# Cluster-masked attention with a SiLU feed-forward layer on one core: eight small DMAs issued from ScalarE's queue in place of SyncE's

## The chip, the cores and the metric

The kernel runs on one core of one Trainium2 chip. The metric is device time in microseconds (us) of a whole execution, given as the median of several runs. Beside the timed runs there is one profiled execution; its times are counted from its first instruction.

Names of engines: PE is TensorE's matmul side and PEld its weight loads, ACT is ScalarE, DVE is VectorE, POOL is GpSimd, SP is SyncE. An engine's name with a q behind it (SPq, ACTq) is its instruction queue, from which it also issues DMAs.

## The reference

Four batches, eight heads, 768 positions, 64 dims per head. Every query and key gets the cluster (of 16) whose normalised centroid it agrees with most, and a query attends only to the keys of its own cluster. The attention output goes through a feed-forward layer with SiLU.

```python
q_assign = np.argmax(np.einsum('bhsd,hcd->bhsc', q_n, c_n), axis=-1)
k_assign = np.argmax(np.einsum('bhsd,hcd->bhsc', k_n, c_n), axis=-1)
mask = q_assign[:, :, :, None] == k_assign[:, :, None, :]
scores = np.where(mask, scale * np.matmul(q, k.transpose(0, 1, 3, 2)), -1000000000.0)
attn = softmax(scores);  x = attn @ v          # x: 3072 x 512
h = x @ w_in;  out = (h / (1 + exp(-h))) @ w_out
```

## The kernel before

**How the mask is made.** A head of a batch is a job; jobs 8 to 15 are the eight heads of batch 1 (names h8 to h15). A job's queries and keys are loaded (`raw`), split into a high and a low half (`hl`: `hi` on ACT, DVE or POOL, `lo` on DVE), and turned over by a DMA transpose (`xpose`, step `ht`) into the tile `ab`, whose 128 rows are the 64 rows of the high half and 64 of the low half. From `ab` PE makes the logits against the centroids (`l` or `L`), DVE takes their maximum (`mx`) and compares (`ge`), which gives a one-hot code for each position. PE turns the codes over (`cd_mm`, step `cm`), and `cd_ev` (step `ce`) takes them out of PSUM into a small tile `cd` of 96 partitions, scaled, with a constant added on the keys' side. From there a DMA of 48 KB moves them into rows 64 to 79 of `ab`. That DMA is the move that the change is about. A single matmul of `ab` by `ab` (`qk_mm`) then gives the score and the mask's penalty at once.

**What waits for a move.** `qk` of a head is the first that reads the moved rows. PE makes the scores of half a head's queries against a third of its keys per step (`qk0` to `qk191`) into `pS`, of which there are two. ACT takes the exponential of each (`ex0` to `ex191`), into `P`. So `qk` of n+2 waits until `ex` of n has read its scores. ACT also does the `tanh` of the feed-forward units (step `t`), some of the evictions, and some `hi`. The feed-forward units (`e`: PE into `ph`, then `t` on ACT, `g` on DVE) and `qk` are interleaved on PE. A `ph` bank comes free when `g` has read it.

**What sets the order.** The order on every engine is that of a list of words, `plan`, written out by hand. Every word is a step, with the engine's letter behind a dot (A ACT, D DVE, P POOL) and a PSUM bank. The list is walked once; each step appends its instructions to its engine's queue, and each queue runs in order. So an instruction that waits holds everything behind it on its engine.

**DMA semaphores.** Each DMA from SP or ACT counts on one of eight semaphores (DMAHW0 to DMAHW7 in the listings), given out in turn over both queues. Before a DMA is issued, its queue waits until the DMA that had the same semaphore before has landed. Here I call such a semaphore a lane.

**The eight moves.** In batch 1 the evictions of jobs 8, 10, 9, 14 and 15 run on ACT and those of 11, 12 and 13 on DVE; all eight moves are issued by SP, among the loads (`raw`, `vn`), the transposes and the stores of results. (Batch 0's moves, which come earlier, are issued by SP as well; batches 2 and 3 make their codes in another way, with moves issued by POOL on line 212.)

Of the kernel before, what the change touches and what calls it, by code (L numbers as in the profile page):

```python
# [29 lines left out]
def kernel(  # L30
# [10 lines left out]
    nc = tc.nc  # L41
    B, H, S, D = q.shape
    HC = centroids.shape[1]
# [39 lines left out]
    raws, hls, abs_ = {}, {}, {}  # L83
# [141 lines left out]
    def cd_ev(job, eng):  # L225
        m = (job.n + 1) // 2
        cd = mp.tile([6 * HC, 256], f16, name="cd", bufs=4)
        psN = psNs.pop(job.name)
        o, i = cd[0 : m * HC], psN[0 : m * HC, 256:512]
        add = 0.0 if job.name[0] == "x" else kadd[0 : m * HC, m - 5 : m - 4]  # L230
        if eng == "A":
            nc.scalar.activation(out=o, in_=i, func=AF.Identity, bias=add, scale=OHV)
        else:
            nc.vector.tensor_scalar(out=o, in0=i, scalar1=OHV, scalar2=add, op0=ALU.mult, op1=ALU.add)  # L234
        nc.sync.dma_start(abs_[job.name][64 : 64 + HC, 0 : 2 * m, :].rearrange("p n c -> p (n c)"), o)

    def ct_mm(job, banks):
        for part, lo_, n, bk in (("q", 6, 3, banks[0]), ("k", 0, 6, banks[1])):
# [365 lines left out]
    def step(op, n, eng, banks):  # L604
# [38 lines left out]
        elif op in ("cm", "xc"):  # L643
            cd_mm(job if op == "cm" else xj, bk)
        elif op in ("ce", "xe"):
            cd_ev(job if op == "ce" else xj, eng)
        elif op == "ct":
            ct_mm(job, banks)
# [86 lines left out]
        ex33 t14 g14 qk34 t8 ex34 qk35 e11.2 e13.3 ht10 g8 wc4 wc5 t11 g11 r12 ex35 t13 g13 qk36 ex36 e10.1 e15.0 qk37  # L735
        pt4.2 qk38 e2.3 t10 ex37 ex38 lo11 pe4.D ht9 r14 pv5.2 g10 t15 nm5 qk39 qk40 t2 ex39 ex40 e7.1 e12.2 t12 ht11
        g15 qk41 ex41 t7 g2 r15 wc6 e9.0 qk42 t9 b0.3 qk43 g7 b1 ex42 wc0 qk44 g12 g9 hi13.D L8.1 ex43 b2 qk45 lo13
        mx8 L10.2 ge8 cm8 mx10 ex44 b3 ex45 ce8.A wc1 ge10 bo0 pv6.1 nm6 qk46 l9.0 ht13 cm10 vl15 ls9 mx9 wc2 ge9 qk47
        hi12.A lo12 vl13 ht12 wc12 b4.3 ce10.A ex46 pt6.2 b5 cm9.0 ex47 hi14.A ce9.A pe6.A lo14 r16 pv7.1 nm7 b6 ht14
        pt5.0 pe5.D qk48 hi15.D lo15 ht15 v10.D pt7.1 pe7.A r17 ex48 b7 bo1 e24.0 e18.1 t24 g24 t18 L11.2 wc8 mx11 g18  # L740
        ge11 e22.3 t22 hi16.P e21.0 t21 g22 v11.D v8.D g21 qk49 qk50 cm11 ce11.D ex49 ex50 l12.3 vl9 ls12 e29.1 r18
        t29 g29 e20.0 t20 g20 e27.2 v13.A mx12 t27 g27 e23.3 ge12 qk51 t23 ex51 l13.1 ls13 qk52 ex52 g23 mx13 e19.0
        t19 e25.2 g19 t25 cm12.1 qk53 ex53 e26.3 g25 v15.D qk54 t26 ex54 ce12.D vl16.P g26 e16.0 t16 e30.2 qk55 ge13
        g16 vl17.P l15.3 ls15 t30 ex55 lo16 r20 qk56 e28.0 t28 ex56 vl14 g30 e17.3 g28 L14.1 qk57 qk58 t17 g17 ex57
        cm13.2 mx14 e31.0 ce13.D ex58 qk59 t31 v9.D mx15 S3 m1.3 ge14 od2 hi17.A ex59 g31 ge15 wc13 pv8.2 cm14 lo17
        r19 ce14.A ht17 qk60 nm8 ex60 S1 qk61 ex61 m7 qk62 ex62 cm15.0 ce15.A wc7 S13 pv9.1 z0 qk63 ex63 S2 nm9 wc14
        v16.D wc9 wc15 wc10 qk64 m11.2 ex64 qk65 m2.0 qk66 ex65 m17 ex66 hi18.P qk67 qk68 lo18 z10 ex67 ht16 vl21.P
        wc11 wc3 S11 v17 S4 m6 pv10.1 ex68 z1 hi20.D qk69 ex69 qk70 ex70 m5 o0 qk71 ex71 l17.0 S12 m16 z2 nm10 z11
        ls17 qk72 vl19.P ht18 vl18.P hi19.A xd8 qk73 l16.0 od1 o3 ex72 r22 r21 ex73 m4 mx17 m15 z12 ls16 mx16 lo19
# [46 lines left out]
    for word in plan:  # L796
        name, *rest = word.split(".")
        eng = rest[0] if rest and rest[0].isalpha() else None
# [31 lines left out]
```

## Time and profile before

| | |
|---|---|
| time, median of 3 runs | 299.18 us (299.0 to 299.66) |
| span of the profiled execution, first to last instruction | 297.9 us |
| what lies around the span (median less span; the profiled execution's own time is not listed beside its span) | 1.3 us |
| PE busy | 288.7 us, 97% |
| PE weight loads busy | 212.6 us, 71% |
| ACT busy | 233.2 us, 78% |
| DVE busy | 223.8 us, 75% |
| POOL busy | 68.7 us, 23% |
| granted TensorE clock | 1.000 |
| moves `ab<-cd` on SP | 16 in the kernel, 8 of them in batch 1 |

How to read it: the share of busy time is an average over the whole kernel. Batch 1's codes are made and moved between 62 and 99 us, so what the change does is read from that stretch. SP does nothing but wait and issue DMAs; its rows show how long its queue was held by each DMA's issue, and a DMA lands some time after.

### The profile page before, as it was taken

To read this page: it belongs to the slowest core of one execution; us is meant where nothing else is said; L and a number is where in the kernel's file an instruction comes from. 1 tells how busy PE (TensorE), PEld (TensorE's weight loads), DVE (VectorE), ACT (ScalarE), POOL (GpSimd) and SP (SyncE) were. 2 spreads that over 40 slices of the span, in tenths; PEclk is the share of its full clock that TensorE was granted. 3 is DMA by queue.
4 is the path that set the end of the run, shared out by engine and by line. 5 is a ranking of instruction groups with operands and counts; after the bars stand their busy time and mean duration, and the time that the engine had idled before them with its cause. 6 is when DMAs were issued, how large, how long until landed. Compare 5 with 4: busy or idle time off the path is not lost.

```text
span 297.9 us, 8577 instructions
## 1 busy us (share of the span) xinstructions
PE 288.7 (97%) x3433; PEld 212.6 (71%) x3433; DVE 223.8 (75%) x489; ACT 233.2 (78%) x406; POOL 68.7 (23%) x124
## 2 busy tenths in 40 slices
PE   7899999999979999999999999999999999999995
PEld 3767766666658887777866887767867886777684
DVE  5898849689979986989467897788656733666663
ACT  5998999965979878999789876898669768964731
POOL 2655804000227001334444024220420000000000
PEclk9999999999999999999999999999999999999999
DMA  6999999999997899795399535867221102211103
GB/s 214 286 256 247 179 201 176 193 247 216 171 300 178 171 176 257 176 151 131 102 202 213 164 66 114 256 165 113 51 89 35 26 2 74 82 29 35 39 19 125
DMA packets 75208, 44.13 MB, mean 148 GB/s; under 512 B 54288, under 2 KB 70960, under 8 KB 75168
## 3 DMA queue, kind: packets, MB, share of 16 engines
q1 hardware_dynamic: 70272, 35.75, 50.3%
q0 software_dynamic: 4608, 7.54, 13.5%
q8 instruction: 27, 0.44, 0.6%
q10 hardware_dynamic: 288, 0.30, 0.3%
q14 instruction: 13, 0.11, 0.1%
HBM read 27.30 MB, written 6.29 MB: 113 GB/s over the span
## 4 chain that ended last, share of the span: by engine, by line
PE 87%; DMA 5%; ACT 3%; DVE 3%; issue 1%; SPq 0%; ACTq 0%
PE ph L390 25%; PE pS L325 20%; PE xb L477 18%; PE pO L342 12%; PE psN L159 4%; PE yb L477 3%; PE po L417 2%; DMA ab<-cd 2%; DMA ab<-hl 1%; DMA raw<-in_q_dram 1%; DVE hl L112 1%; PE wb L477 1%; ACT P L330 1%; ACT hl L103 1%; PE pTq L135 1%
## 5 line engine op out<-in xcount | busy, mean ns | idle before, releaser
L330 ACT ACTIVATE P<-pS 128x768 f16<-128x768 f32 x192 | 151.0, 815 | 18.8 <-PE pS L325 17.4
L390 PE MATMUL ph<-xt,win_s 128*128 128x384 f16 x512 | 96.1, 326 | 0.0
L405 DVE SCALAR_TENSOR_TENSOR gt<-tn,ph 128x384 f16<-128x384 f32 x128 | 68.2, 549 | 31.9 <-ACT tn L402 31.0
L325 PE MATMUL pS<-ab 128*128 128x384 f16 x384 | 86.7, 326 | 2.2 <-DMA ab<-cd 1.6
L402 ACT ACTIVATE tn<-ph 128x384 f32<-128x384 f32 x128 | 61.6, 499 | 13.9 <-PE ph L390 10.5
L390 PEld LDWEIGHTS <-win_s 128*128 128x128 f16 x512 | 49.4, 98 | 31.0 <-issue 0.3
L325 PEld LDWEIGHTS <-ab 128*128 128x128 f16 x384 | 34.2, 98 | 18.3 <-DMA ab<-cd 2.2
L342 PEld LDWEIGHTS <-P 128*128 128x128 f16 x1152 | 39.8, 97 | 3.8 <-DVE cd L234 0.4
L342 PE MATMUL pO<-vt,P 128*128 128x65 f16 x1152 | 41.2, 193 | 0.0
L477 PEld LDWEIGHTS <-gt 128*128 128x128 f16 x352 | 34.1, 98 | 6.5
L112 DVE SCALAR_TENSOR_TENSOR hl<-raw,hl 128x768 f16<-128x768 f32 (+3 forms) x35 | 32.0, 916 | 0.8 <-ACT hl L103 0.5
L105 POOL TENSOR_SCALAR hl<-raw 128x768 f16<-128x768 f32 (+1 forms) x9 | 19.5, 2167 | 47.2 <-DVE gt L405 30.7
L477 PEld LDWEIGHTS <-s 128*128 128x128 f16 x264 | 25.5, 98 | 4.7
L199 POOL TENSOR_SCALAR od<-od 128x96 f16<-128x96 f16 x16 | 8.4, 526 | 63.3 <-DVE od L192 63.2
L499 ACT ACTIVATE ot<-xb 128x256 f32<-128x256 f32 x33 | 12.7, 385 | 12.9 <-PE xb L477 12.6
L477 PE MATMUL xb<-wout_s,gt 128*128 128x256 f16 x176 | 22.6, 273 | 0.0
L159 PEld LDWEIGHTS <-ab 128*128 128x128 f16 x544 | 18.9, 97 | 4.1 <-DMA ab<-hl 0.5
L477 PE MATMUL xb<-wc,s 128*128 128x256 f16 x160 | 20.7, 272 | 0.0
L159 PE MATMUL psN<-stk,ab 128*128 128x16 f16 (+1 forms) x544 | 20.1, 184 | 0.1
L354 DVE TENSOR_TENSOR xn<-pO,zr 128x384 f16<-128x384 f32 x32 | 17.8, 557 | 1.1
L490 DVE TENSOR_TENSOR s<-gt 128x1024 f16<-128x1024 f16 x22 | 15.5, 712 | 1.3 <-PE xb L477 1.0
L212 POOL DMA_DIRECT2D ab<-cdt x16 | 9.0, 564 | 19.8 <-PE pS L325 5.2
(93 smaller groups left out, 258.2 us busy)
## 6 DMA issues: line engine op xcount, KB each, us to landing
raw<-in_k_dram SPq DMA_DIRECT2D x31, 192.0 KB, 3.9
raw<-in_q_dram SPq DMA_DIRECT2D x24, 192.0 KB, 3.5
out_dram<-ot SPq DMA_DIRECT2D x18, 256.0 KB, 2.9
vn<-in_v_dram SPq DMA_DIRECT2D x19, 192.0 KB, 4.7
vn<-in_v_dram POOLq DMA_DIRECT2D x13, 192.0 KB, 3.4
win_s<-in_moe_w_in_dram POOLq DMA_DIRECT2D x8, 256.0 KB, 6.8
wout_s<-in_moe_w_out_dram POOLq DMA_DIRECT2D x4, 512.0 KB, 9.2
out_dram<-ot SPq DMA_DIRECT2D x12, 128.0 KB, 1.8
```

Source lines behind the costliest of these rows:

```text
L105: nc.gpsimd.tensor_scalar(out=o, in0=i, scalar1=QS, scalar2=None, op0=ALU.mult)
L112: nc.vector.scalar_tensor_tensor(out=hl[:, s, 1, :], in0=raws[job.name][:, s, :], scalar=QS, in1=hl[:, s, 0, :], op0=ALU.mult, op1=ALU.sub ...
L159: nc.tensor.matmul(L[:, n % 2, :, n // 2], ab[:, i, :], stk[:, job.groups[i // 3][0], x : x + w], start=(x == 0), stop=(x + w == 2 * HC),)
L325: nc.tensor.matmul(pS[:, e, 0:HALF], abs_[kj.name][:, kn, :], rhs, start=True, stop=True)
L330: nc.scalar.activation(out=P, in_=pst.pop(u)[:, :, 0:HALF], func=AF.Exp, bias=0.0, scale=ESC)
L342: nc.tensor.matmul(o[:, (2 * t + h) * VW : (2 * t + h + 1) * VW], Ps[i + h, c, j // 2][:, j % 2, ts(t, 128)], vtb[(i + h) % 13][:, j, 0:VW ...
L354: nc.vector.tensor_tensor(out=xn, in0=ov[:, :, 0:D], in1=zr.unsqueeze(2).to_broadcast([128, 2 * NM, D]), op=ALU.mult)
L390: nc.tensor.matmul(ph[:, 0:HALF], win_s[:, r, ts(fb, 128)], xts[b, c][:, r, :], start=(r == 0), stop=(r == NR - 1))
L402: nc.scalar.activation(out=tn, in_=phs[b, c, fb][:, 0:HALF], func=AF.Tanh, bias=0.0, scale=0.5)
L405: nc.vector.scalar_tensor_tensor(out=gt[:, fb, NM * c : NM * c + NM, :].rearrange("p t n -> p (t n)"), in0=tns.pop((b, c, fb)), scalar=1.0 ...
L477: nc.tensor.matmul(o, self.lhs(l, f), self.rhs(r, f), start=(f == 0 and opens), stop=(f == HB - 1), skip_group_check=True)
L490: nc.vector.tensor_tensor(out=o, in0=a, in1=b_, op=op)
```

## The change

A move is issued by the engine that its step's letter names: B evicts on ACT and issues on ACT, C evicts on DVE and issues on ACT. The eight steps of batch 1 get these letters; batch 0's keep theirs. The place in the list stays, so the move stands on ACT's queue where the step stands among ACT's other work.

```diff
-        if eng == "A":
+        if eng in "AB":
             nc.scalar.activation(out=o, in_=i, func=AF.Identity, bias=add, scale=OHV)
         else:
             nc.vector.tensor_scalar(out=o, in0=i, scalar1=OHV, scalar2=add, op0=ALU.mult, op1=ALU.add)
-        nc.sync.dma_start(abs_[job.name][64 : 64 + HC, 0 : 2 * m, :].rearrange("p n c -> p (n c)"), o)
+        (nc.scalar if eng in "BC" else nc.sync).dma_start(abs_[job.name][64 : 64 + HC, 0 : 2 * m, :].rearrange("p n c -> p (n c)"), o)
...
-        ge11 e22.3 t22 hi16.P e21.0 t21 g22 v11.D v8.D g21 qk49 qk50 cm11 ce11.D ex49 ex50 l12.3 vl9 ls12 e29.1 r18
+        ge11 e22.3 t22 hi16.P e21.0 t21 g22 v11.D v8.D g21 qk49 qk50 cm11 ce11.C ex49 ex50 l12.3 vl9 ls12 e29.1 r18
...
-        cm13.2 mx14 e31.0 ce13.D ex58 qk59 t31 v9.D mx15 S3 m1.3 ge14 od2 hi17.A ex59 g31 ge15 wc13 pv8.2 cm14 lo17
-        r19 ce14.A ht17 qk60 nm8 ex60 S1 qk61 ex61 m7 qk62 ex62 cm15.0 ce15.A wc7 S13 pv9.1 z0 qk63 ex63 S2 nm9 wc14
+        cm13.2 mx14 e31.0 ce13.C ex58 qk59 t31 v9.D mx15 S3 m1.3 ge14 od2 hi17.A ex59 g31 ge15 wc13 pv8.2 cm14 lo17
+        r19 ce14.B ht17 qk60 nm8 ex60 S1 qk61 ex61 m7 qk62 ex62 cm15.0 ce15.B wc7 S13 pv9.1 z0 qk63 ex63 S2 nm9 wc14
```

In the same way ce8, ce10 and ce9 go from A to B, and ce12 from D to C. How this moves the instructions is best seen at two places. The names of tiles are numbered: `ab_1594` is the tile of job 12, `ab_1675` of job 14, `ab_1688` of job 15; `cd_1602` and `cd_1622` hold the codes of jobs 10 and 9.

The first place is SP's queue around the transposes of jobs 12 and 14, before:

```order
L264 DMA vn_1592<-in_v_dram 128x384 [waits DMAHW6_49]
L121 DMA_TRANSPOSE ab_1594<-hl_1589 128x12x128 [waits DMAHW7_49,DVE_49]
L235 DMA ab_1258<-cd_1602 16x6x256 [waits DMAHW0_49,Activation_49]
L235 DMA ab_1313<-cd_1622 16x6x256 [waits DMAHW1_49,Activation_49]
L92 DMA raw_1627<-in_q_dram 128x384 [waits DMAHW2_49]
L92 DMA raw_1627<-in_k_dram 128x384 [waits DMAHW3_49]
L121 DMA_TRANSPOSE ab_1675<-hl_1620 128x12x128 [waits DMAHW4_49,DVE_49]
L121 DMA_TRANSPOSE ab_1688<-hl_1685 128x12x128 [waits DMAHW5_49,DVE_49]
```

and now:

```order
L264 DMA vn_1592<-in_v_dram 128x384 [waits DMAHW7_49]
L121 DMA_TRANSPOSE ab_1594<-hl_1589 128x12x128 [waits DMAHW0_49,DVE_49,PE_49]
L92 DMA raw_1627<-in_q_dram 128x384 [waits DMAHW2_49,DMAHW1_49]
L92 DMA raw_1627<-in_k_dram 128x384 [waits DMAHW3_49]
L121 DMA_TRANSPOSE ab_1675<-hl_1620 128x12x128 [waits DMAHW4_49,DVE_49]
L121 DMA_TRANSPOSE ab_1688<-hl_1685 128x12x128 [waits DMAHW5_49,DVE_49,PE_49]
```

The two moves are gone from between job 12's transpose and the loads; the transpose of job 14 still has lane DMAHW4.

The second place is ACT's queue around the exponentials of steps 49 and 50 (`P_1784`, `P_1786`), before:

```order
L402 ACTIVATE tn_1758<-ph_1753 128x384 [waits PE_49,Activation_49]
L402 ACTIVATE tn_1767<-ph_1762 128x384 [waits DVE_49,PE_49]
L330 ACTIVATE P_1784<-pS_1773 128x768 [waits PE_49]
L330 ACTIVATE P_1786<-pS_1776 128x768 [waits PE_49]
L402 ACTIVATE tn_1813<-ph_1805 128x384 [waits DVE_49,PE_49]
```

and now:

```order
L402 ACTIVATE tn_1758<-ph_1753 128x384 [waits PE_49]
L402 ACTIVATE tn_1767<-ph_1762 128x384 [waits DVE_49,PE_49]
L235 DMA ab_1386<-cd_1781 16x6x256 [waits DMAHW7_49,DMAHW4_49,DVE_49]
L330 ACTIVATE P_1784<-pS_1773 128x768 [waits PE_49]
L330 ACTIVATE P_1786<-pS_1776 128x768 [waits PE_49]
L402 ACTIVATE tn_1813<-ph_1805 128x384 [waits PE_49,Activation_49]
```

Job 11's move (`ab_1386<-cd_1781`) now stands on ACT ahead of these two exponentials. It waits for DVE's eviction into `cd_1781`, for lane DMAHW7 (job 11's transpose) and for lane DMAHW4, on which the DMA before it is job 14's transpose `ab_1675<-hl_1620`.

More of the change, by code (lines that the diff above doesn't have):

```diff
@@ L737 @@
         g15 qk41 ex41 t7 g2 r15 wc6 e9.0 qk42 t9 b0.3 qk43 g7 b1 ex42 wc0 qk44 g12 g9 hi13.D L8.1 ex43 b2 qk45 lo13
-        mx8 L10.2 ge8 cm8 mx10 ex44 b3 ex45 ce8.A wc1 ge10 bo0 pv6.1 nm6 qk46 l9.0 ht13 cm10 vl15 ls9 mx9 wc2 ge9 qk47
-        hi12.A lo12 vl13 ht12 wc12 b4.3 ce10.A ex46 pt6.2 b5 cm9.0 ex47 hi14.A ce9.A pe6.A lo14 r16 pv7.1 nm7 b6 ht14
+        mx8 L10.2 ge8 cm8 mx10 ex44 b3 ex45 ce8.B wc1 ge10 bo0 pv6.1 nm6 qk46 l9.0 ht13 cm10 vl15 ls9 mx9 wc2 ge9 qk47
+        hi12.A lo12 vl13 ht12 wc12 b4.3 ce10.B ex46 pt6.2 b5 cm9.0 ex47 hi14.A ce9.B pe6.A lo14 r16 pv7.1 nm7 b6 ht14
         pt5.0 pe5.D qk48 hi15.D lo15 ht15 v10.D pt7.1 pe7.A r17 ex48 b7 bo1 e24.0 e18.1 t24 g24 t18 L11.2 wc8 mx11 g18
-        ge11 e22.3 t22 hi16.P e21.0 t21 g22 v11.D v8.D g21 qk49 qk50 cm11 ce11.D ex49 ex50 l12.3 vl9 ls12 e29.1 r18
+        ge11 e22.3 t22 hi16.P e21.0 t21 g22 v11.D v8.D g21 qk49 qk50 cm11 ce11.C ex49 ex50 l12.3 vl9 ls12 e29.1 r18
         t29 g29 e20.0 t20 g20 e27.2 v13.A mx12 t27 g27 e23.3 ge12 qk51 t23 ex51 l13.1 ls13 qk52 ex52 g23 mx13 e19.0
-        t19 e25.2 g19 t25 cm12.1 qk53 ex53 e26.3 g25 v15.D qk54 t26 ex54 ce12.D vl16.P g26 e16.0 t16 e30.2 qk55 ge13
+        t19 e25.2 g19 t25 cm12.1 qk53 ex53 e26.3 g25 v15.D qk54 t26 ex54 ce12.C vl16.P g26 e16.0 t16 e30.2 qk55 ge13
         g16 vl17.P l15.3 ls15 t30 ex55 lo16 r20 qk56 e28.0 t28 ex56 vl14 g30 e17.3 g28 L14.1 qk57 qk58 t17 g17 ex57
-        cm13.2 mx14 e31.0 ce13.D ex58 qk59 t31 v9.D mx15 S3 m1.3 ge14 od2 hi17.A ex59 g31 ge15 wc13 pv8.2 cm14 lo17
-        r19 ce14.A ht17 qk60 nm8 ex60 S1 qk61 ex61 m7 qk62 ex62 cm15.0 ce15.A wc7 S13 pv9.1 z0 qk63 ex63 S2 nm9 wc14
+        cm13.2 mx14 e31.0 ce13.C ex58 qk59 t31 v9.D mx15 S3 m1.3 ge14 od2 hi17.A ex59 g31 ge15 wc13 pv8.2 cm14 lo17
+        r19 ce14.B ht17 qk60 nm8 ex60 S1 qk61 ex61 m7 qk62 ex62 cm15.0 ce15.B wc7 S13 pv9.1 z0 qk63 ex63 S2 nm9 wc14
         v16.D wc9 wc15 wc10 qk64 m11.2 ex64 qk65 m2.0 qk66 ex65 m17 ex66 hi18.P qk67 qk68 lo18 z10 ex67 ht16 vl21.P
```

## The prediction

> **What bounds the kernel now.** I read the page first, then the waits and the chain of waits between 50 and 120 us, then the timelines of PE, SP, ACT and DVE there.
>
> ```profile
> PE 288.7 (97%) x3433; PEld 212.6 (71%) x3433; DVE 223.8 (75%) x489; ACT 233.2 (78%) x406; POOL 68.7 (23%) x124
> PE 87%; DMA 5%; ACT 3%; DVE 3%; issue 1%; SPq 0%; ACTq 0%
> ```
>
> PE is busy for 97% of the span and makes up 87% of the chain that ends last. So a microsecond that PE idles is a microsecond of the kernel, and the question is only where the change adds or removes idle time of PE. One row of the waits between 57 and 101 us (who waited for whom: us in total, times, longest) names the moves, and the chain and PE's timeline give its place:
>
> ```profile
> PE pS L325 <- DMA ab<-cd: 1.6, 1, 1.6
> ...
> 82.05 5.36 DMA ab<-cd
> ...
> 83.83 1.46 PE L390 MATMUL ph<-xt,win_s 128*128 128x384 f16 x8
> 85.13 0.76 PE L159 MATMUL psN<-stk,ab 128*128 128x16 f16 x24
> 87.46 0.82 PE L325 MATMUL pS<-ab 128*128 128x384 f16 x4 [1.57 <-DMA ab<-cd]
> ```
>
> SP issues job 11's move at 82.05; it lands 5.36 us later, at 87.41, and qk57 starts at 87.46 after 1.57 us of idle PE. That is all that the eight moves cost PE today: **the most that the change can win is 1.57 us**. Why so late? The codes had been evicted long before:
>
> ```profile
> 75.41 0.47 DVE L234 TENSOR_SCALAR cd<-psN,kadd 96x256 f16<-96x256 f32 x1
> ...
> 65.02 0.43 SPq L92 DMA_DIRECT2D raw<-in_k_dram  x1
> 65.94 0.60 SPq L235 DMA_DIRECT2D ab<-cd  x1
> 66.64 0.61 SPq L423 DMA_DIRECT2D out_dram<-ot  x1
> ...
> 70.38 2.22 SPq L121 DMA_TRANSPOSE ab<-hl  x1
> 72.70 1.26 SPq L235 DMA_DIRECT2D ab<-cd  x2
> 74.02 0.58 SPq L92 DMA_DIRECT2D raw<-in_q_dram  x1
> 74.65 0.50 SPq L92 DMA_DIRECT2D raw<-in_k_dram  x1
> 75.25 5.13 SPq L121 DMA_TRANSPOSE ab<-hl  x2
> ```
>
> The eviction ended at 75.88, and SP got to its move at 82.05, behind the transposes of jobs 14 and 15 and three more DMAs. Issued from another queue the move can start 5 us sooner. **The gain of 1.57 us I take as certain, if ACT itself does not become late.**
>
> **What the change adds to ACT.** Eight issues, each standing in ACT's queue, and whatever they wait for.
>
> *Price of one issue.* SP's own moves in this stretch, and ACT's only two DMAs, at the start:
>
> ```profile
> L235 SPq DMA_DIRECT2D ab<-cd x8: 562/584/860, 65.9 to 94.5; - x8
> ...
> 0.72 0.41 ACTq L92 DMA_DIRECT2D raw<-in_k_dram  x1
> 0.73 0.39 SPq L544 DMA_DIRECT2D craw<-in_centroids_dram  x1
> ...
> 1.65 1.28 ACT L559 ACT_TABLE_LOAD   x1 [1.65 <-PEq L814]
> ```
>
> The same move takes 0.56 to 0.86 us on SP; ACT's load took 0.41. I take 0.57, since it is the same transfer, with 0.41 and 0.86 as ends. ACT's table load follows its two issues at 1.65, and nothing of ACT runs beside them, so I count an issue as time in which ACT does nothing else.
>
> *Jobs 8, 10 and 9* (62 to 70 us):
>
> ```profile
> 64.84 0.47 ACT L232 ACTIVATE cd<-psN,kadd 96x256 f16<-96x256 f32 x1 [1.56 <-DVE xn L354]
> 69.94 0.49 ACT L372 ACTIVATE xt<-px 128x384 f16<-128x384 f16 x1 [1.77 <-PE px L363]
> ```
>
> A move after ACT's own eviction costs the 0.09 us by which the next instruction now starts before the eviction's end, about 0.05 for the semaphore, and 0.57: 0.7 us. Job 8's is covered by the 1.56 us of idle ACT at 64.84. Those of jobs 10 and 9 lie ahead of the 1.77 us of idle ACT, which covers 1.4. What is not covered is that job 14's `hi` on ACT, and with it `lo` on DVE, comes 0.7 later; I reckon 0.4 us on PE at the next units, and this is swallowed by the next wait.
>
> *Job 11*, the dear one. ACT reaches this move after the tanh that ends at 74.49; before, exponentials 49 and 50 followed there at once:
>
> ```profile
> 74.00 0.49 ACT L402 ACTIVATE tn<-ph 128x384 f32<-128x384 f32 x1
> 74.39 1.51 ACT L330 ACTIVATE P<-pS 128x768 f16<-128x768 f32 x2
> ...
> 82.49 1.00 ACT L402 ACTIVATE tn<-ph 128x384 f32<-128x384 f32 x2
> ...
> 78.11 0.51 PE L159 MATMUL psN<-stk,ab 128*128 128x32 f16 x12
> 83.24 0.54 DVE L405 SCALAR_TENSOR_TENSOR gt<-tn,ph 128x384 f16<-128x384 f32 x1
> ```
>
> The move waits for DVE's eviction (75.88 before, some 76.3 with the 0.4 above) and, by its lane, for the landing of job 14's transpose. When is that? SP has lost three moves ahead of it. The store at 66.64 can follow the load that ends at 65.45, 1.1 us sooner; the transpose of job 12 then starts at 69.25 and ends at 71.5; the two moves (1.3 us) are gone, so the loads run from 71.5 to 72.65, and job 14's transpose is issued at 72.75 instead of 75.25. From issue to landing (transposes issued or running between 57.5 and 82 us: least, median, most; then job 14's alone; then job 12's by the chain):
>
> ```profile
> DMA to landing us min/median/max: 4.1/5.1/11.1
> ...
> DMA to landing us min/median/max: 5.7/5.7/5.7
> ...
> 70.38 4.40 DMA ab<-hl
> ```
>
> The ends are 4.1 and 5.7; I take 4.4, that of the transpose which now stands closest ahead of it in the same backlog. It lands at 77.15 (76.85 to 78.45). So ACT idles from about 74.9 to 77.15, issues for 0.57, and exponential 49 starts at 77.75, **3.36 us later than before**. Behind it wait both score buffers (qk51 needs ex49's) and the tanh of unit 29, whose bank PE needs at 78.11 for job 13's logits. From there to the tanh at 82.49 ACT had 8.1 us, of which 0.4 is idle: no room to catch up. Job 12's move, whose eviction on DVE ends at about the end of ex54, adds 0.6. So that tanh starts at 77.75 + 7.7 + 0.6 = 86.05, 3.55 late. PE's units at 83.83 (row above) wait for its gate on DVE (83.24, some 0.2 us after that tanh ended): they come 3.35 late, at 87.2. PE works 2.06 us from there to 85.89, so qk57 starts at 89.25; job 11's move landed long before. Against 87.46 this is **+1.8 us, the 1.57 us that are won already taken off**.
>
> *Jobs 13, 14 and 15*:
>
> ```profile
> 88.44 0.48 DVE L234 TENSOR_SCALAR cd<-psC,kadd 96x256 f16<-96x256 f32 x1 [1.32 <-PE psC L221]
> 88.00 1.51 ACT L330 ACTIVATE P<-pS 128x768 f16<-128x768 f32 x2 [1.74 <-PE pS L325]
> 91.50 0.47 ACT L232 ACTIVATE cd<-psN,kadd 96x256 f16<-96x256 f32 x1 [0.19 <-PE psN L221]
> 91.88 2.29 ACT L330 ACTIVATE P<-pS 128x768 f16<-128x768 f32 x3
> 94.06 0.46 ACT L232 ACTIVATE cd<-psC,kadd 96x256 f16<-96x256 f32 x1
> 92.83 0.49 PE L325 MATMUL pS<-ab 128*128 128x384 f16 x2
> 90.00:95.00 5.00, 5.00 (x97) 4.29 (x95) 4.96 (x12) 4.71 (x9) 4.70 (x7) 1.00 0.62 165
> ```
>
> Job 13's move stands between exponentials 57 and 58 (88.00 and 88.70). It needs DVE's eviction, 88.92, so ex58 starts at 88.92 + 0.05 + 0.57 = 89.54: 0.84 late. Jobs 14 and 15 cost 0.7 each as above: 2.24 in all. ACT is busy 4.71 of 5 us in the last row and PE 5.00, so ACT's own slack up to 95 is about 0.4. PE's scores at 92.83 need the first of the three exponentials from 91.88, which ends about 92.65: a lead of 0.2. **What reaches PE is 2.24 - 0.4 - 0.2 = 1.6 us.**
>
> After 97 us nothing is changed, and PE, which had no idle time to speak of, gives nothing back.
>
> **The sum.** 1.8 + 1.6 = 3.4 us, on the profiled span of 297.9 us: 301.3. The median of the runs lies 1.28 above that span; 302.6, of which I take off 0.1 for the loads that SP starts sooner: **302.5 us**. With the cheap ends (transpose at 76.85, issue 0.41 on the five moves from job 11 on) the loss is 3.4 - 0.3 - 0.8 = 2.3, and if PE has 0.8 more lead than I see, 1.5: 300.7. With the dear ones (78.45, issue 0.86) it is 3.4 + 1.3 + 1.45 = 6.1: 305.2.
>
> **Rivals.**
>
> *ACT and SP hinder each other in issuing.* If only one DMA can be set up at a time, an ACT issue stands behind SP's current one, and SP's are long here:
>
> ```profile
> 62.17 2.08 SPq L121 DMA_TRANSPOSE ab<-hl  x1
> ```
>
> Job 8's issue would then wait until 64.25, which the idle ACT just covers; job 11's about 0.6 behind job 15's transpose; the last four some 0.3 each behind loads: 1.8 more, 304.3 us. For it: SP issues nearly without a gap from 58 to 86 us. Against it: at 0.72 and 0.73 both queues issued a load at once, and each took its usual 0.4 us. [...]
>
> *Faster: ACT goes on while its DMA waits.* If the waiting move is set aside and only its 0.57 us or less holds the engine, in the shade of a running exponential, the 1.57 us are won and nothing is lost: 297.6 us. It decides from the point where ACT loses less than about 1.6 us in total. For it: ACT is busy 78% on the average, and PE's own queue runs ahead by loading weights early. Against it: each queue runs in order, and SP's queue shows no DMA passing a waiting one.
>
> *A draw.* Job 14's transpose lands before the eviction (76.3 instead of 77.15), issues cost 0.41 and ACT's lateness is mostly covered between 88 and 97: a loss of 1.4 to 1.9 against the gain of 1.57, about 299.3 us.
>
> That the change does not do what it says can be ruled out: the order of ACT's queue shows the eight issues.
>
> **How the numbers follow.** Forecast 0.61, exclusive issue 0.17, faster 0.13, draw 0.09. About 0.2% (0.6 us) is what a measurement of this kernel can tell from no change. The first two are slower, the third faster; of the draw 0.07 is within 0.2% and 0.02 slower. Faster 0.13, same 0.07, slower 0.80. The forecast's own range is 300.7 to 305.2, which also holds the exclusive issue. To leave out no more than 2 in 10 the range goes down through the draw: 299.0 to 305.2.
>
> **What would show it.** Right: ACT idle for some 2 us or more before the exponentials near 75 us, ended by a DMA `ab<-hl`, with DMA issues of about 0.57 us on ACT's queue; PE's wait for `ab<-cd` near 86 us gone; in its place PE waits on ACT or DVE near 78 to 87 us, and short waits for ACT's exponentials between 91 and 98. SP's transpose of job 14 issued near 72.7. Wrong: the ACT wait ended by DVE's eviction alone (then the loss is nearer 2.5), issues on ACT much longer than 0.86 us beside SP's transposes (the exclusive issue), or exponentials that run on while a move waits (faster). If the loss between 88 and 97 us is missing, PE had more lead over ACT than the rows let me see.

## The result, and the profile after

The changed kernel takes **303.59 us** (median of 4 runs, 303.05 to 307.61) against 299.35 us for the kernel before beside it (299.0 to 299.66): ratio **1.014, 95% interval 1.0105 to 1.0174**. It is slower. The interval leaves out the run of 307.61 us, which is the profiled one and had a lower granted clock (0.994) than the other three (0.998 to 1.0); where this lower clock comes from is a question for the experiments.

The page of the changed kernel, its busy line and its chain, against PE 97% and 87% before:

```profile
PE 291.3 (95%) x3433; PEld 213.1 (70%) x3433; DVE 223.2 (73%) x489; ACT 233.6 (76%) x406; POOL 67.5 (22%) x124
PE 77%; DMA 7%; ACT 6%; DVE 5%; issue 3%; ACTq 1%; POOL 0%; DVEq 0%; POOLq 0%
```

PE has lost ten points of the chain to DMA, ACT, DVE and the issue gaps, though ACT has no more work than before (233.6 against 233.2 us). ACT was not filled; it was stopped. These rows of the changed kernel's waits between 57 and 105 us (us in total, times, longest) say by what, and who was stopped in turn:

```profile
DVE gt L405 <- ACT tn L402: 8.7, 7, 5.3
ACT P L330 <- DMA ab<-hl: 5.2, 1, 5.2
PE pS L325 <- ACT P L330: 4.4, 4, 2.8
PE psN L159 <- DVE gt L405: 1.2, 1, 1.2
```

The row for `PE pS` waiting for `ab<-cd`, 1.6 us before, is gone. In its place PE waits for ACT and DVE. The place is in ACT's timeline (start, length, engine and line, what it did, idle time before it and what ended it):

```profile
75.27 0.49 ACT L402 ACTIVATE tn<-ph 128x384 f32<-128x384 f32 x1 [0.16 <-PE ph L390]
80.30 0.58 ACTq L235 DMA_DIRECT2D ab<-cd  x1
80.93 1.51 ACT L330 ACTIVATE P<-pS 128x768 f16<-128x768 f32 x2 [5.16 <-DMA ab<-hl]
```

The chain has job 14's transpose there, from issue to landing:

```profile
74.25 5.98 DMA ab<-hl
```

And PE's timeline has what follows from it:

```profile
81.79 0.48 PE L325 MATMUL pS<-ab 128*128 128x384 f16 x2 [2.84 <-ACT P L330]
83.46 0.80 PE L159 MATMUL psN<-stk,ab 128*128 128x32 f16 x12 [1.19 <-DVE gt L405]
...
98.26 0.48 PE L325 MATMUL pS<-ab 128*128 128x384 f16 x2 [0.77 <-ACT P L330]
100.09 0.48 PE L325 MATMUL pS<-ab 128*128 128x384 f16 x2 [0.47 <-ACT P L330]
103.58 0.48 PE L325 MATMUL pS<-ab 128*128 128x384 f16 x2 [0.27 <-ACT P L330]
```

After the tanh that ends at 75.76, ACT does nothing until 80.30 (the 5.16 us of the row run on to 80.93, so they hold the issue too), because job 11's move stands at the head of its queue and waits for the semaphore of job 14's transpose, which SP issued at 74.25 and which landed 5.98 us later. The issue itself takes 0.58 us. Then PE waits 2.84 us for exponential 49 and 1.19 us for the gate that the late tanh releases, 0.4 us more at 91.27 for a gate behind job 12's move, and later three times for an exponential (1.51 us in all), where the moves of jobs 13 to 15 stand.

One thing was in no step of the prediction. Here are four stretches of PE in the changed kernel, each about 3.41 us long and laid so that they meet where the clock changes (length, PE busy, granted clock, DMA share, GB/s):

```profile
76.45:79.87 3.42, 2.50 (x16) 1.00 1.35 112
79.87:83.28 3.41, 0.48 (x2) 1.00 1.06 306
83.28:86.69 3.41, 3.23 (x21) 0.50 0.75 265
86.69:90.10 3.41, 3.41 (x26) 1.00 0.00 0
```

Right after the stretch in which PE was idle for 2.93 us, TensorE ran at half its clock for 3.41 us. Two matmuls of the scores took 0.83 us there (at 84.07) and 0.49 us at full clock (at 87.10). By that I estimate that the 3.23 us of work in this stretch cost about 3.23 / 2 = 1.6 us more than at full clock. In the profile of the kernel before, the clock is 1.00 in every window from 57 to 110 us.

### The profile page after: what moved, and what is told of

Read it like the earlier page. It is cut to its first block, busy times and chain, and to the rows that moved or that the text cites. A ratio compares the mean times of both kernels' runs of the same rounds, so it can differ in the third digit from the quotient of the medians.

```text
span 305.5 us, 8571 instructions
## 1 busy us (share of the span) xinstructions
PE 291.3 (95%) x3433; PEld 213.1 (70%) x3433; DVE 223.2 (73%) x489; ACT 233.6 (76%) x406; POOL 67.5 (22%) x124
## 4 chain that ended last, share of the span: by engine, by line
PE 77%; DMA 7%; ACT 6%; DVE 5%; issue 3%; ACTq 1%; POOL 0%; DVEq 0%; POOLq 0%
PE ph L390 25%; PE xb L477 17%; PE pS L325 16%; PE pO L342 9%; PE yb L477 3%; PE psN L159 3%; ACT P L330 3%; DMA vn<-in_v_dram 3%; DMA ab<-hl 2%; DMA ab<-cd 2%; DVE hl L112 1%; PE wb L477 1%; PE po L417 1%; ACT hl L103 1%; DMA raw<-in_q_dram 1%
## 5 line engine op out<-in xcount | busy, mean ns | idle before, releaser
L390 PE MATMUL ph<-xt,win_s 128*128 128x384 f16 x512 | 97.1, 328 | 0.5 <-DVE gt L405 0.4
L105 POOL TENSOR_SCALAR hl<-raw 128x768 f16<-128x768 f32 (+1 forms) x9 | 18.3, 2033 | 43.3 <-DVE gt L405 26.8
L168 DVE TENSOR_REDUCE L<-psN 128x192 f32<-128x384 f32 x20 | 11.1, 554 | 3.6 <-PE psN L159 3.4
```

The lines of the kernel that those rows point to most:

```text
L105: nc.gpsimd.tensor_scalar(out=o, in0=i, scalar1=QS, scalar2=None, op0=ALU.mult)
L390: nc.tensor.matmul(ph[:, 0:HALF], win_s[:, r, ts(fb, 128)], xts[b, c][:, r, :], start=(r == 0), stop=(r == NR - 1))
```

## The experiments

In the variants a move can be given its engine by job, and the lines behind the move's stand eight lower: L243 is the move, L338 the exponential, L413 the gate, L410 the tanh. Each was compared with the kernel before on the same chip: 298.72 us in the first set (`whole`, `only11`, `first3`, `last4`), 299.12 in the second (`lane`, `place`, `warm`, `sp1`), 298.9 in the third (`whole_b`, `warm2`, `late3`, `sp2`). The sets ran on different chips, so their ratios are compared rather than their times.

### The change once more: `whole`

The changed kernel, unaltered.

> The changed kernel once more, for more times and another profile. Theory (the wait): ACT idles about 5 us ahead of exponential 49, ended by the landing of job 14's transpose on the shared lane; 303 to 304 us. Rival (the issues): the eight issues of 0.57 us on ACT make the loss, 4.6 us less what is covered, and the long wait is only where they happen to show; the same time. Second rival (the clock): the TensorE clock falls to half after PE's idle time in every execution, and without it the loss would be 2 us or less.

Measured: 307.38 us (305.62 to 308.17), ratio 1.0284 (1.0236 to 1.0331). This is twice the loss of the first comparison and misses the 303 to 304 us that were expected. In its profile the mechanism is the same: ACT idles for 4.83 us, the issue included, and the wait is ended by `ab<-hl`. The chain has job 14's transpose at the same place, and it landed at 80.28:

```profile
75.08 5.20 DMA ab<-hl
```

PE's windows there, with the columns as above:

```profile
80.86:84.27 3.41, 1.25 (x17) 1.00 0.78 198
84.27:87.68 3.41, 3.41 (x14) 0.50 0.88 328
```

Here too PE ran at half clock, for the 3.41 us after a stretch in which it was busy for 1.25 us. PE also waits 0.7 us for job 12's transpose in this execution, because SP's queue was late ahead of it. So the size of the loss differs from one execution of the same code to the next, and what differs had to be found. (The expectation's second rival, a loss of 2 us or less where the clock stays whole, falls with the first comparison: its three executions at full clock lost about 4.2 us.)

### Parts alone: `only11`, `first3`, `last4`, `late3`

```diff
+    ON_ACT = {"h11"}                          # only11
+    ON_ACT = {"h8", "h10", "h9"}              # first3
+    ON_ACT = {"h12", "h13", "h14", "h15"}     # last4
+    ON_ACT = {"h13", "h14", "h15"}            # late3
```

Here `ON_ACT` holds the jobs whose move ACT issues; the others stay with SP.

> Job 11's move alone is issued by ACT, the other seven by SP as before. Its lane is now that of job 9's move, which lands at 76.1, and not that of job 14's transpose. Theory (the wait): ACT idles from 74.5 to 76.1, issues for 0.57, exponential 49 starts near 76.75, 2.4 us late; that costs PE 1.8 us up to qk57, and the 1.57 us of waiting for the move are won: 299.0 to 300.0. Rival (the issues): one issue of 0.57 against a gain of 1.57: 298.3.

Measured: 299.53 us, ratio 1.0035 (1.0008 to 1.0061), in the expected range. DVE's and ACT's timelines in `only11`, and the two moves that SP issued before (their issues, then their time to landing with ACT's as the longest):

```profile
76.39 0.47 DVE L234 TENSOR_SCALAR cd<-psN,kadd 96x256 f16<-96x256 f32 x1
...
77.43 0.67 ACTq L243 DMA_DIRECT2D ab<-cd  x1
78.14 1.51 ACT L338 ACTIVATE P<-pS 128x768 f16<-128x768 f32 x2 [2.66 <-PE ph L398]
...
L243 SPq DMA_DIRECT2D ab<-cd x2: 562/588/613, 73.6 to 74.3; - x2
DMA to landing us min/median/max: 3.0/3.1/5.0
```

Alone, this move shares its semaphore with job 9's move, which SP issued at 74.3 and which landed some 3 us later, near 77.4. DVE's eviction had ended at 76.86. So here too the end of ACT's wait fits the landing on the shared lane, half a us behind the eviction (the row names the last of PE's matmuls that exponential 49 needed, but those were long done). ACT idles for 2.66 us instead of 5.16, and PE's wait for `ab<-cd` is gone; what is left is a small loss, not a gain. Even without the transpose, the move costs ACT more than it wins for PE.

> The moves of jobs 8, 10 and 9 alone are issued by ACT. Theory (the wait): they are covered by ACT's idle time except for 0.4 us at the units near 70 us, and since SP loses three issues, job 11's move leaves SP about 2.4 us sooner (79.7 instead of 82.05) and PE no longer waits for it: 0.4 lost, 1.5 won, 298.2. Rival (the issues): three issues of 0.57 us cost PE 1.7 us: 299.5 with the gain, 301 without it.

Measured: 298.39 us, ratio 0.9977 (0.9942 to 1.0011), close to the expected 298.2. The profile has no wait of PE at all between 57 and 105 us: with three issues fewer, SP reaches job 11's move at 79.37. So what the three moves cost is offset by what they win, and no loss can be measured, as the prediction had it.

> The moves of jobs 12, 13, 14 and 15 alone are issued by ACT. Theory: job 12's issue makes ACT 0.6 us late, which is hidden by PE's wait for job 11's move, and this wait stays; jobs 13 to 15 cost PE 1.6 us between 88 and 97 us: 300.9. Rival (PE has more lead over ACT than the rows show): 299.4, no change.

Measured: 301.71 us, ratio 1.0109 (1.0067 to 1.0152), which is 3.3 us for four moves, twice the 1.6 that were expected. Its profile has PE waiting 1.2 us for exponentials, 0.6 us for `ab<-cd` and 0.2 us for `ab<-hl` between 57 and 105 us, 2.0 us in all; it does not show where the rest of the loss comes from.

> Only the moves of jobs 13, 14 and 15 are issued by ACT; jobs 8 to 12 stay with SP. The prediction's term is 1.6 us for these three, against a kernel that keeps its wait of 1.57 us for job 11's move: 300.7 at a median of 299.1 before. With jobs 12 to 15 the loss was 3.0 us (299.72-us kernel to 301.71 at 298.7, ratio 1.0109). Theory (the term was undersized, since ACT hands its delay on to PE through DVE's layer norms too): 301.0 to 302.0 at 299.1, so that job 12's move has 0.3 to 1.1 us of the 3.0. Rival (job 12's move carries the difference): 300.4 to 300.9.

Measured: 301.24 us (300.23 to 301.91 in six executions, and one of 305.1 with a granted clock of 0.994), ratio of the six 1.0067 (1.0042 to 1.0092): 2.0 us, 1.3 to 2.7 with the interval. PE's only wait between 57 and 105 us in `late3`:

```profile
PE pS L333 <- ACT P L338: 1.6, 3, 0.9
```

PE waits 1.6 us for the exponentials, which is the prediction's figure for these three moves. The interval of the times holds it too, and also holds my later guess of 2 us or more; these runs can't tell the two apart. The difference to `last4`, about 1.3 us, goes with job 12's move; no trace shows how.

This profile shows something else. All that SP issues ahead of job 11's move is as in the kernel before, and yet SP gets there sooner, at 79.40 instead of 82.05:

```profile
79.40 0.61 SPq L243 DMA_DIRECT2D ab<-cd  x1
```

In this execution PE doesn't wait for `ab<-cd`, and in that of `last4`, with the same queue ahead of the move, it waits 0.6 us. So the wait of 1.57 us in the profile of before is not there in full in every execution.

### The wait taken from job 11's move: `lane` and `place`

`lane`: all eight moves on ACT, and three loads (step `vl9` and the two of job 18) issued by POOL, whose DMAs do not count on the lanes: in the trace of the kernel before, those of SP and ACT are on eight semaphores and POOL's 41 on eight others. The turns of the lanes shift, and job 11's move shares its lane with an older load instead of job 14's transpose.

```diff
-            load(job)
+            load(job, (nc.gpsimd, nc.gpsimd) if eng == "P" else (nc.sync, nc.sync))
...
-        ... ex49 ex50 l12.3 vl9 ls12 e29.1 r18
+        ... ex49 ex50 l12.3 vl9.P ls12 e29.1 r18.P
```

> All eight moves are issued by ACT, as in the change, but three loads that SP issued between job 14's transpose and job 11's move (v of head 9, and q and k of job 18) are issued by POOL. So the lanes shift: job 11's move waits for the load of job 16's queries (landed near 76) instead of job 14's transpose, job 12's for job 9's move. Theory (the wait): ACT's wait ends at DVE's eviction near 76.5, exponential 49 starts near 77, PE idles about 1 us there instead of 3 or more, and the clock stays whole: 301.5 to 303 us, some 5 us less than the change in the same job. Rival (the issues): the eight issues are still there, so the time stays within 1 us of the change's, near 307.

Measured: 301.81 us (301.63 to 302.3), ratio 1.0082 (1.0059 to 1.0106), in the expected range, and the clock is 0.999 or 1.0 in all 9 executions. ACT's timeline in `lane`:

```profile
76.30 0.57 ACTq L243 DMA_DIRECT2D ab<-cd  x1
76.92 1.51 ACT L338 ACTIVATE P<-pS 128x768 f16<-128x768 f32 x2 [1.98 <-PE ph L398]
```

And PE's, with all of its idle time from 75 to 85 us:

```profile
79.45 0.51 PE L159 MATMUL psN<-stk,ab 128*128 128x32 f16 x12 [1.01 <-DVE gt L413]
```

With the shared lane away, ACT goes on as soon as DVE's eviction has ended (76.26). It idles for 1.98 us instead of 5.16, and the 2.84 us that PE waited for exponential 49 are gone. Not all of that is the lane: SP issued job 14's transpose early in this execution, at 72.06. With the 4.96 to 5.98 us that it took from issue to landing in the three traces of the change, I estimate that it landed at 77.0 to 78.0, so waiting for it would have held ACT 0.7 to 1.7 us longer. The eight moves on ACT then cost 2.5 us, where the three comparisons of the change gave 4.2, 8.5 and 8.1, and the nine times lie within 0.7 us. The variant alters three issues beside the lane; but since ACT's wait for the transpose is what is missing in its trace, I take the lane for the larger part of the loss. The next variant alters nothing but the place of one issue.

`place`: all eight on ACT, and job 11's move issued behind exponential 52, when the transpose is about to land.

```diff
-        ... qk51 t23 ex51 l13.1 ls13 qk52 ex52 g23 mx13 e19.0
+        ... qk51 t23 ex51 l13.1 ls13 qk52 ex52 mv11.A g23 mx13 e19.0
```

> All eight moves are issued by ACT, but job 11's move stands behind exponential 52 instead of ahead of exponential 49; its lane is still that of job 14's transpose. Theory (the wait): the two scores and four tanhs ahead of it cover the transpose's landing, exponential 49 starts as before the change, and what is left is 0.6 us of issue there plus the cost of jobs 12 to 15 (3 us as measured alone, less what they share with the 1.57 us won): 300.5 to 302. Rival (the issues): the same eight issues, near 307.

Measured: 301.09 us (300.6 to 302.42), ratio 1.0056 (1.0033 to 1.0079), as expected. The move goes out at 80.06, between exponential 52 and a tanh, with ACT running up to it:

```profile
79.18 1.51 ACT L338 ACTIVATE P<-pS 128x768 f16<-128x768 f32 x2
80.06 0.57 ACTq L243 DMA_DIRECT2D ab<-cd  x1
80.73 0.87 ACT L410 ACTIVATE tn<-ph 128x384 f32<-128x384 f32 x2
```

With the same eight issues and the same lane, the loss is 1.7 us. So nearly the whole harm of job 11's move is its waiting, and its price on ACT's queue is small; the rival that the issues make the loss falls. What is left in `place` is close to what `late3` costs.

### The half clock: `warm`, `whole_b`, `warm2`

If the lower clock follows from PE's idle time, work that keeps PE busy there must keep the clock. Both variants are the changed kernel with matmuls ahead of the scores of step 51 (`qk51`); they multiply zeros, and nothing reads what they give.

```diff
+        elif op == "warm":
+            t = phs[0, 1, 7]
+            for _ in range(n):
+                nc.tensor.matmul(t[:, 384:512], zz[:, 0:128], zz[:, 0:128], start=True, stop=True)
...
-        ... e23.3 ge12 qk51 t23 ex51
+        ... e23.3 ge12 warm20 qk51 t23 ex51
```

> The change, with 20 matmuls of 128 columns of zeros added on PE ahead of qk51, where PE idles while ACT waits; they write columns that nothing reads. Theory (the clock follows the idle time): the TensorE clock no longer falls to half for 3.41 us, ACT's wait stays: about 1.7 us less than the change in the same job, 305 to 306. Rival (the clock has another cause): half clock for 3.41 us again, 307 to 308.

Measured: 307.03 us (304.49 to 308.15), ratio 1.0229 (1.0164 to 1.0294). The attempt missed its aim: 20 of these matmuls are worth only 1.28 us, and PE still idles. From PE's timeline in `warm`:

```profile
78.47 1.28 PE L624 MATMUL ph<-zz 128*128 128x128 f16 x20
81.89 0.80 PE L333 MATMUL pS<-ab 128*128 128x384 f16 x2 [2.14 <-ACT P L338]
```

And its windows:

```profile
78.37:81.78 3.41, 1.38 (x22) 1.00 1.24 205
81.78:85.19 3.41, 2.42 (x18) 0.50 0.97 298
85.19:88.60 3.41, 3.41 (x14) 0.50 0.28 101
```

So it says nothing on the cause. It does show the half clock lasting two windows where the first of them again holds idle time: 2.42 us of work at half clock did not bring the full clock back, where 3.23 us did in the first profile. The third set ran the changed kernel and a filler of the right size beside each other, with `warm45` in the place of `warm20`.

> The changed kernel once more, for comparison with the others on the same chip. Two earlier looks gave 303.59 (4 runs) and 307.38 us. If PE's lower clock after its longest idle time is a matter of when the 3.41-us windows fall, some executions have it and some not: between 303 and 307.5 us against the kernel before. In the profile, ACT idle for 4.8 to 5.2 us ahead of exponential 49, and PE idle for some 2 to 3 us ahead of the scores of unit 51.

> The changed kernel with 45 matmuls of 128 columns (0.064 us each by the run with 20, so 2.9 us) put before qk51, where PE waits for exponential 49. They add work that nothing reads, and take about the place of the idle time. Theory (the lower clock follows from PE's idle share in the 3.41-us window before): PE is idle for less than 1.6 us in any such window, the clock stays at 1.0, and the time falls to 302 to 304 us, at least 2 us below the run of the changed kernel beside it. Rival (the lower clock belongs to something else that the change does at 80 us, such as ACT's or the DMA's stand): the half clock stays near 82 us and the time is 305 to 308. If the fillers themselves end later than exponential 49, PE's scores come later by that, some 0.3 us.

Measured: `whole_b` 306.87 us (304.97 to 307.98), ratio 1.0271 (1.0236 to 1.0306), clock 0.989 to 0.994 in all four executions; `warm2` 305.04 us (303.49 to 306.63), ratio 1.0198 (1.0147 to 1.0248), clock 0.999 to 1.0 in all four. PE's windows around the place in `whole_b`:

```profile
77.16:80.58 3.42, 1.26 (x7) 1.00 1.09 191
80.58:83.99 3.41, 3.33 (x21) 0.50 1.06 350
```

PE's timeline in `warm2`, with no idle time from the fillers to the scores of step 51 and job 13's logits:

```profile
78.22 2.68 PE L624 MATMUL ph<-zz 128*128 128x128 f16 x45
80.73 0.49 PE L333 MATMUL pS<-ab 128*128 128x384 f16 x2
81.05 0.51 PE L159 MATMUL psN<-stk,ab 128*128 128x32 f16 x12
```

And its windows:

```profile
79.41:82.82 3.41, 3.41 (x50) 1.00 0.96 311
82.82:86.23 3.41, 3.41 (x29) 1.00 0.18 67
```

With PE's idle time filled by useless work, and nothing else changed, the half clock is gone from every execution: it follows from PE's idle time, which is the theory. The rival (something else at 80 us) falls. The time fell by 1.8 us at the median, about one half-clock window, but not to the expected 302 to 304, and the two sets of four times overlap, so the clock shows the cause and the time does not. Part of that is the filler's own price: it ended at 80.90, and the scores of step 51 came at 80.73 instead of 78.99 in `whole_b`, of which 0.4 us (81.05 against 80.66 for job 13's logits) was not covered. The rest lies within a spread of 3 us between executions. So `warm2` still loses 5.9 us by its ratio at full clock: the half clock is one part of the loss beyond the forecast, and not the whole of it.

How much idle time it takes can be told from these traces only between two figures. In the 3.41 us before the clock fell, PE had worked for 0.48 us in the changed kernel's first profile, 1.25 in `whole`, 1.26 in `whole_b` and 1.38 in `warm`. Where PE worked for 1.84 us or more in every stretch of 3.41 us (the kernel before between 57 and 110 us, idle for at most 1.57 of them), the clock did not fall.

The executions of the changed kernel, ordered by the granted clock of each:

| granted clock | times, us |
|---|---|
| 0.998 to 1.0 | 303.05, 303.56, 303.62 |
| 0.994 (one window of half clock, by the three traces at hand) | 304.97, 305.62, 307.36, 307.61 |
| 0.989 (two windows, by the mean; a trace shows it for `warm` only) | 306.55, 307.19, 307.39, 307.98, 308.17 |

One window is 3.41 / 2 = 1.7 us of 305, or 0.0056 of the mean clock, which fits the column. Why some executions escape is not shown: of those at 0.998 to 1.0 there is no trace, and that it is a matter of when the windows fall stays a guess of the expectation for `whole_b`. None of the 59 executions of the kernel before in the three sets has a clock below 0.998. But 0.994 also stands beside one of `late3`'s seven executions (305.1 us) and one of `sp1`'s ten (299.53 us, all moves on SP), which have no trace either, so the half clock is no mark of job 11's move alone.

### Another way to the same gain: `sp1` and `sp2`

All moves stay with SP, and what stands ahead of job 11's move on SP's queue is put behind it: the two loads of job 17 (`sp1`, by moving the word `r17`), and in `sp2` job 15's transpose (`ht15`) as well.

```diff
-        ... hi15.D lo15 ht15 v10.D pt7.1 pe7.A r17 ex48 ... cm11 ce11.D ex49
+        ... hi15.D lo15 ht15 v10.D pt7.1 pe7.A ex48 ... cm11 ce11.D r17 ex49        # sp1
+        ... hi15.D lo15 v10.D pt7.1 pe7.A ex48 ... cm11 ce11.D ht15 r17 ex49        # sp2
```

> All moves stay on SP; only the two loads of job 17 are moved behind job 11's move in SP's queue. Theory: the move is issued at 80.9 instead of 82.05 and lands before 86, so PE's wait of 1.57 us goes, for nothing in exchange: 297.8. Rival (the transfer is what is late, not the issue): it lands no sooner, no change.

> All eight moves stay on SP; job 11's stands ahead of job 15's transpose and of job 17's two loads in SP's queue. If PE's only loss in the kernel before is its 1.57 us before qk57, and job 15's transpose and job 17's loads can come later without anyone waiting for them, the time falls by 1.0 to 1.6 us: 297.5 to 298.1 at 299.1 before. Moving job 17's loads alone gave 0.9969 (297.9 to 298.6 here). Rival (the transpose of job 15, now issued some 1 to 2 us later, is waited for by PE in turn): no better than 298.5, with a wait of PE for ab<-hl in the profile.

Measured: `sp1` 298.76 us, ratio 0.9969 (0.9943 to 0.9995); `sp2` 297.97 us, ratio 0.9967 (0.9948 to 0.9987). Both beat the kernel before by 0.3%, that is by 0.9 and 1.0 us, with intervals that end just short of no change. The middle of neither is the whole 1.57 us, though `sp1`'s interval holds it. `sp1`'s profile has no wait of PE between 57 and 105 us. In `sp2` SP issues job 11's move at 78.31:

```profile
78.31 0.60 SPq L243 DMA_DIRECT2D ab<-cd  x1
```

PE's one wait there, in the slowest of the ten executions, is for an earlier job's move; there is none for `ab<-hl`, so the rival falls:

```profile
69.97 0.50 PE L333 MATMUL pS<-ab 128*128 128x384 f16 x2 [1.00 <-DMA ab<-cd]
```

## Why the prediction was right, and where it was short

**The sign and the mechanism: right.** The loss comes from ACT standing in order behind a DMA that waits for job 14's transpose by a shared semaphore. The trace shows the wait (ACT idle for 5.16 us with the issue, ended by `ab<-hl`). `place` and `lane` take it away, and the loss falls from 4.2 to 8.5 us to 1.7 and 2.5. `only11`, with another DMA on the lane, has 2.66 us in its place.

**The stretch from 62 to 90 us, predicted +1.8: right without the clock, when the transpose is as early as I took it.** Two executions of the changed kernel can be measured against before by the same matmuls (the weighted values `pO` of a head). In PE's timeline of before:

```profile
62.74 1.26 PE L342 MATMUL pO<-vt,P 128*128 128x65 f16 x36
...
90.08 1.26 PE L342 MATMUL pO<-vt,P 128*128 128x65 f16 x36
```

In the changed kernel's first profile:

```profile
63.61 1.26 PE L342 MATMUL pO<-vt,P 128*128 128x65 f16 x36
...
95.78 1.26 PE L342 MATMUL pO<-vt,P 128*128 128x65 f16 x36
```

In `whole_b`:

```profile
62.61 1.26 PE L342 MATMUL pO<-vt,P 128*128 128x65 f16 x36
...
93.01 1.26 PE L342 MATMUL pO<-vt,P 128*128 128x65 f16 x36
```

And the chain's piece for job 14's transpose in `whole_b`:

```profile
72.48 4.96 DMA ab<-hl
```

| us | predicted | changed kernel, first profile | `whole_b` |
|---|---|---|---|
| later than before at 62.7, ahead of the first move | 0 | 0.87 | -0.13 |
| added up to the `pO` at 90.08 | 1.8 | 4.83 | 3.06 |
| of this, half clock (half of PE's work in the window) | 0 | 1.6 | 1.7 |
| of this, the rest | 1.8 | 3.2 | 1.4 |
| PE's idle time from there to 110 (`whole_b`: 0.28, 0.95 and 0.27 in three windows) | 1.6 | 1.5 | 1.5 |
| what is left of the span's difference | 0 | 0.4 | 0.5 |
| span | +3.4 | +7.6 | +4.9 |

In `whole_b` the transpose landed at 77.44, close to the 77.15 of the prediction, and the rest is 1.4 us. In the first profile it landed at 80.23. Taking off what each was late or early at 62.7, that is 79.36 against 77.57, or 1.8 us later, and the rest is 1.8 us more. So **the landing was mis-sized for some executions**: issued at 72.48, 74.25 and 75.08 in the three profiles (predicted 72.75), and 4.96, 5.98 and 5.20 us to landing (predicted 4.4, ends 4.1 and 5.7). The ends of the range held two of the three latencies, but I took the lateness of SP's queue ahead of the transpose as fixed, from one execution.

**The step that failed is one that is not there: the clock.** The sum counts PE's idle time only. In the three traces of the change, idle time that fell close together, 2.2 to 2.9 us of it in one window of 3.41 us, also halved TensorE's clock for the next 3.41 us, at 1.6 to 1.7 us each by my estimate (half of PE's work in it); in `warm`, 2.0 us of it halved the clock for 6.82 us. Two comparisons of three came out at 1.027 and 1.028, which is 307.3 and 307.7 us at the median of before (299.18 times the ratio), beyond the range's upper end of 305.2, and all eight of their executions had one or two such windows by their mean clock. The first, 303.59, lies inside the range because three of its four executions escaped; that is luck, and not a merit of the sum. Nor is the clock all that is missing from the sum: without half clock `warm2` still lost 5.9 us against the forecast 3.4, some 0.4 of it for the filler. Its profiled execution, the fastest of the four, has a span of 301.4 us, 3.5 more than before's 297.9 and so as forecast; the three slower ones have no trace. The late landing above accounts for 1.8 us in one execution; the rest stays open.

**The gain of 1.57 us, taken as certain: too much.** The wait for `ab<-cd` did go. But `late3` shows an execution without it though SP does the same ahead of the move, and taking it away won only 0.9 and 1.0 us by the ratios of `sp1` and `sp2`. The profiled execution of before seems to have been above the median itself: its span is 297.9 us, and an execution of before in the third set with that span took 300.09, against a median of 299.18. With a gain of 0.95 in place of 1.57 the prediction's sum would be 4.0 us, and the time 303.1, which is where the three executions without half clock lie (303.05 to 303.62).

**Jobs 8, 10 and 9, covered: right, as far as it can be told.** `first3` gives 0.9977 (0.9942 to 1.0011), a win of 0.7 us, in which the gain for job 11's move is already counted. If that gain is the 0.9 to 1.0 us of `sp1` and `sp2`, some 0.3 us is left for the three moves, less than the interval's width.

**Jobs 13 to 15, 1.6 us: right by the profiles** (PE's idle time of 1.5, 1.5 and 1.6 us in three of them), and not refuted by `late3`'s time. Job 12's move was put at 0.6 us inside the chain of job 11; the difference of `last4` and `late3`, 1.3 us across two sets, makes it rather more, though `last4`'s profile does not show where.

**The price of an issue, 0.57 us: right, and the exclusive issue fell.** ACT's issue of its first move in the changed kernel:

```profile
63.45 0.68 ACTq L235 DMA_DIRECT2D ab<-cd  x1
```

And what SP was issuing at the same time:

```profile
62.46 1.69 SPq L121 DMA_TRANSPOSE ab<-hl  x1
```

ACT's issue began at 63.45 and ended at 64.13, all of it within SP's transpose (62.46 to 64.15), and took 0.1 us more than the 0.57 of the others. An issue that had to wait for the end of SP's could not have ended before it.

**ACT goes on while its DMA waits: false.** It did nothing from 75.76 to 80.30. **The draw: false**; only `only11`, with one move on ACT, came near it.

## What to carry to other kernels

Before a DMA is moved to a computing engine's queue, list what that DMA waits for, its semaphore's last user included, because here that wait became idle time of the engine: the issue cost 0.57 us, and the wait and the issue together up to 5.58 us of ACT's time (4.83 and 5.16 in `whole` and in the changed kernel's first profile, 5.58 in `warm`). Put the issue where its wait is already over (`place`), or reorder the queue it stands in (`sp1`, `sp2`), which here won 0.3% where the other queue lost 1.4% or more. When PE is the bound, look at how close together its idle time falls: 2.2 to 2.9 us of it in one 3.41-us window, even in two pieces of 1.0 and 1.2 us (`whole_b`), cost another 1.6 to 1.7 us of halved clock by my estimate, and 2.9 us in `warm`, where the next window held idle time too ((2.42 + 3.41) / 2).

## What the runs showed of the hardware that I had not expected

- TensorE's granted clock fell to 0.50 for 3.41 us (three traces of the change) or 6.82 us (`warm`) after a window of 3.41 us in which PE worked for 0.48 to 1.38 us. With matmuls on zeros that nothing reads (`warm2`) the mean clock was 0.999 or 1.0 in four executions of four, against 0.989 to 0.994 without them (`whole_b`).
- The same code differs by up to 5 us over twelve executions on three occasions (303.05 to 308.17). In the three traces, job 14's transpose was issued at 72.48 to 75.08 and landed at 77.44 to 80.28, and the clock fell in all three after the idle time that followed; that this makes up the whole spread is not shown.
- Taking the wait of 1.57 us away on SP's side won only some 1 us, most likely because that wait is not in full in every execution: the same queue reached job 11's move at 82.05 in one profile and at 79.40 in another (`late3`).
